# How a start-up path and two transposes are carried: DMA or TensorE, in an attention kernel with a SiLU feed-forward

## The chip, the cores and the metric

The kernel runs on one core of a Trainium2 chip. The metric is the device time of one execution in microseconds. A time is the median of several runs, and a profile is one execution recorded by the hardware profiler.

Engines are called by short names: PE (TensorE, matrix products and transposes into PSUM), DVE (VectorE), ACT (ScalarE), POOL (GpSimd) and SP (SyncE, which here only issues DMAs). Each engine works through its own list of instructions in order, and semaphores tie the lists together. PEld is the weight load of PE, which overlaps its products.

## The reference

Inputs r, k, v have the shape (4 batches, 8 heads, 768 steps, 48), w and u (8 heads, 48); the feed-forward weights w_in are 384x2048 and w_out 2048x384, all in float32.

```
state = 0
for t in range(S):
    cur   = einsum('bhd,bhe->bhde', u * k[t], v[t])
    y[t]  = einsum('bhd,bhde->bhe', r[t], state + cur)
    state = w[:, :, None] * state + einsum('bhd,bhe->bhde', k[t], v[t])

x = y.transpose(0, 2, 1, 3).reshape(B * S, H * D)
h = x @ w_in
out = (h * sigmoid(h)) @ w_out
```

So there is a decay w and a bonus u, one number for each head and channel, that every unit of work needs; then a feed-forward of two layers over 3072 tokens.

## The kernel before

The 768 steps are cut into 6 chunks of 128, and a *unit* is one chunk of one batch: 24 units, unit i being chunk i // 4 of batch i % 4. A unit goes through these steps (functions in the code):

- `load(i)`: three DMAs on SP's queue bring r, k and v of the unit into slot i % 6 (`NIN` is 6), time on the partitions. A later unit's load reuses the slot.
- `p1(i)` (units 0 to 3) or `p1t` and `p1d` (later units): PE transposes r and k so that channels lie on the partitions, and DVE multiplies them by powers of w (`lamR`, `lamK`) into `rk`.
- `nat_ku`, `nat_rk` (POOL), `bonus_sum` (DVE), `bonus_vu` (POOL) or `bonus_act` (ACT): the bonus term, the row sum of r·k·u times v, called `vu`.
- `p2(i)`: PE multiplies k by r for the even and odd heads (`ae`, `ao`), and DVE masks the result into `am`.
- `p3y`, `p3e`: PE forms y from `am`, v and the state; DVE adds `vu` and writes `y16` in float16.
- `sums`, `state`, `half_state`, `nat_kc`, `r16`: the state that is carried to the next chunk.
- `p4(i)`: y16 is turned so that channels lie on the partitions (`xT`), as the feed-forward needs them.

The feed-forward of a chunk is `l1` (16 column tiles of w_in, three products each, then Silu on ACT into `gT`) and `l2` (per batch 16 products in four parts, a DVE copy `osb`, a store on SP's queue). These pieces stand in a list, `fillers`, and `fill(n)` takes pieces worth n from it and puts them between the steps of a unit, so that PE has work while the attention's short steps wait for each other. For chunk 1 the first layer is done in two halves: units 4 and 5, then units 6 and 7 (`l1s(1, 2, 4)`, entered behind unit 7's steps).

The order of the instructions on every engine is the order in which the program is written out by hand (`manual_schedule`). The ramp of units 0 to 5 is written step by step (lines 413 to 558); from unit 6 on there is a loop (lines 559 to 594).

What matters for the start: w is read as columns, channels on the partitions, by two DMAs of 4-byte elements (line 83). DVE doubles it seven times into all its powers (lines 141 to 148). u is read by one DMA that repeats its 384 numbers on all 128 partitions (line 87), between k and v of unit 0. `spin` issues products of zeros that nothing reads. The four parts of w_in and the two of w_out are brought by POOL's queue, which converts them to float16 (`win_part`, `wout_part`); the first one is held back by a POOL copy `gate` that reads r of unit 1 (line 424), and the loads of units 4 and 5 by a POOL memset in their slot (line 451).

What matters for units 6 and 7: `p4` turns y16 by three PE transposes and an ACT copy for units 0 to 7 (lines 334 to 338), and by a DMA transpose on SP's queue from unit 8 on (line 331). In the loop, units 6 and 7 issue the loads of units 12 and 13 ahead of `p3y` (lines 570 and 571); later units issue theirs behind `p4` (lines 580 and 581).

Of the kernel before, what the change touches and what calls it, by code (L numbers as in the profile page):

```python
# [8 lines left out]
FP = mybir.dt.float32  # L9
# [6 lines left out]
def kernel(  # L16
# [47 lines left out]
    def load(i, mid=None):  # L64
        if i >= NU:
            return
        sc, b = unit(i)
        for t, src in ((rin, r), (kin, k), (vin, v)):
            if t is vin and mid:
                mid()  # L70
            nc.sync.dma_start(out=t[i % NIN][:, :, 0:D],
                              in_=src[b, :, sc * C:sc * C + C, :]
                              .rearrange("h t d -> t h d"))

    wcol = cst.tile([PR, NP], FP)
    u_bc = cst.tile([128, H, D], FP)
    junk = cst.tile([128, 512], F16)
    nc.vector.memset(junk, 0.0)  # L80
    nc.vector.memset(wcol[32:64, :], 1.0)
    for j, e in ((0, nc.sync), (1, nc.scalar)):
        e.dma_start(out=wcol[64 * j:64 * j + D, :],
                    in_=bass.AP(tensor=w.tensor, offset=D * j, ap=[[1, D], [PW, NP]]))

    def load_u():
        nc.sync.dma_start(out=u_bc.rearrange("t h d -> t (h d)"),
                          in_=bass.AP(tensor=u.tensor, offset=0, ap=[[0, 128], [1, HD]]))

    load(0, mid=load_u)  # L90
    for i in range(1, B):
        load(i)
    for t in (rin, kin):
# [25 lines left out]
    def spin(n, t=None):  # L119

        if t is None:
            t = ps.tile([128, 512], FP, name="spin", tag="t", bufs=5)
        else:
            t = t.rearrange("s p t -> s (p t)")
        for _ in range(n):
            nc.tensor.matmul(t, junk[:, 0:128], junk, start=True, stop=True)

    spin(10)
    lamC = cst.tile([128, H, D], FP)

    def to_rows(dst, cols):

        t = ps.tile([128, NP, 2, 64], FP, name="rows", tag="t", bufs=5)
        for p in range(NP):
            nc.tensor.transpose(t[:, p, :, :].rearrange("t j d -> t (j d)")[:, 0:PR],
                                cols(p), ident[0:PR, 0:PR])
        nc.scalar.copy(out=dst.rearrange("t (p j) d -> t p j d", j=2), in_=t[:, :, :, 0:D])


    wT = wcol  # L140
    nc.vector.tensor_copy(out=pi[:, 0:NP, 1:2], in_=wT.unsqueeze(2))
    nc.vector.reciprocal(out=pi[:, NP:2 * NP, 1:2], in_=wT.unsqueeze(2))
    n = 1
# [22 lines left out]
    def nat_ku(i):  # L166
        L = live.setdefault(i, {})
        L["ku"] = wrk.tile([128, H, D], FP, name="ku")
        nc.gpsimd.tensor_tensor(out=L["ku"], in0=kin[i % NIN][:, :, 0:D], in1=u_bc,  # L169
                                op=ALU.mult)  # L170

    def nat_rk(i):
        L = live[i]
        L["rku_f"] = wrk.tile([128, H, D], FP, name="rku_f")
        nc.gpsimd.tensor_tensor(out=L["rku_f"], in0=rin[i % NIN][:, :, 0:D], in1=L["ku"],  # L175
                                op=ALU.mult)
# [6 lines left out]
    def bonus_sum(i):  # L183
        L = live[i]
        L["rku"] = wrk.tile([128, H], FP, name="rku", bufs=3)
        nc.vector.tensor_reduce(out=L["rku"], in_=L["rku_f"], axis=mybir.AxisListType.X,  # L186
                                op=ALU.add)
# [12 lines left out]
            nc.scalar.activation(out=L["vu"][:, h, :], in_=vin[i % NIN][:, h, :],  # L200
                                 func=AF.Copy, scale=L["rku"][:, h:h + 1])

    def p1(i, spins=0):
        n = i % NIN
        L = live.setdefault(i, {})
        tr = ps.tile([128, NP, C], FP, name="tr", tag="t", bufs=5)
        tk = ps.tile([128, NP, C], FP, name="tk", tag="t", bufs=5)
        spin(spins, tr)
        for t, src in ((tr, rin), (tk, kin)):
            flat = src[n].rearrange("p h d -> p (h d)")  # L210
            for p in range(NP):
                nc.tensor.transpose(t[0:PR, p, :], flat[:, 128 * p:128 * p + PR], ident)
        rk = wrk.tile([PR, 2, NP, C], FP, name="rk")
        L["rT"] = rk[:, 0]
        L["kT"] = rk[:, 1]
        step = NP // 2 if i == 0 else NP
        for q in range(0, NP, step):
            q = slice(q, q + step)
            for x, t, lam_ in (("rT", tr, lamR), ("kT", tk, lamK)):
                nc.vector.tensor_tensor(out=L[x][:, q], in0=t[0:PR, q], in1=lam_[:, q],  # L220
                                        op=ALU.mult)

    def p1t(i):

# [100 lines left out]
    def p4(i):  # L325
        sc, b = unit(i)
        L = live[i]
        if sc not in xts:
            xts[sc] = wrk.tile([128, NQ, B, C], F16, name="xT", bufs=3)
        if i >= 2 * B:  # L330
            nc.sync.dma_start_transpose(out=xts[sc][:, :, b, :],
                                        in_=L["y16"].rearrange("p h d -> p (h d)"))
            return
        yT = ps.tile([128, NQ, C], F16, name="yT", tag="t", bufs=5)
        yf = L["y16"].rearrange("p h d -> p (h d)")
        for q in range(NQ):
            nc.tensor.transpose(yT[:, q, :], yf[:, 128 * q:128 * q + 128], ident16)
        nc.scalar.copy(out=xts[sc][:, :, b, :], in_=yT)
# [58 lines left out]
            f()  # L397


    zero = junk[0:PR, 0:HD].rearrange("r (p c) -> r p c", p=NP)  # L400
    gate = cst.tile([128, 1], FP)

    def win_part(c0, c1):
        nc.gpsimd.dma_start(out=win[:, :, c0:c1],  # L404
                            in_=moe_w_in[:, c0:c1].rearrange("(q p) n -> p q n", p=128))
# [4 lines left out]
            in_=moe_w_out[1024 * g:1024 * g + 1024, :].rearrange("(f p) n -> p f n", p=128))  # L410


    p1(0)
    nat_ku(0)
    nat_rk(0)
    p2(0)
    nat_v(0)
    lamCT = cst.tile([PR, NP, C], FP)
    for p in range(NP):
# [3 lines left out]
    nc.scalar.copy(out=st[0], in_=zero)  # L423
    nc.gpsimd.tensor_copy(out=gate, in_=rin[1][:, 0, 0:1])
    win_part(0, 512)
    p1(1, spins=1)
    bonus_sum(0)
    nat_ku(1)
# [3 lines left out]
    to_rows(lamC, lambda p: lamCT[:, p, :])  # L432
    bonus_act(0)
    nc.scalar.copy(out=st[1], in_=zero)
    bonus_sum(1)
    bonus_vu(1)
    win_part(512, 1024)
    p2(1, spins=2)
    p3e(0)
    spin(4)  # L440
# [118 lines left out]
    for i in range(B + 2, NU):  # L559
        sc, b = unit(i)  # L560
        if i == B + 2:
            p2(i, nxt=i + 1)
        bonus_sum(i)
        bonus_vu(i)
        if i > B + 2:
            p2(i, nxt=i + 1 if i + 1 < NU else None)
        fill(2)
        if i + 1 < NU:
            front(i + 1)
        if NIN <= i < 2 * B:  # L570
            load(i + NIN)
        fill(1)
        p3y(i)
        p3e(i)
        if sc < NCH - 1:
            sums(i)
            state(i)
        fill(2)
        p4(i)
        if i >= 2 * B:  # L580
            load(i + NIN)
        if i + 1 < NU:
            r16(i + 1)
        if i == B + 2:
            half_state(3)
        fill(1)
        if sc == 1:
            half_state(b)
        fill(1 if sc in (2, 3) else 2)
        if b == B - 1:  # L590
            if sc == 1:
                fillers.extend(l1s(1, 2, 4) + l2s(1))
            else:
                fillers.extend(l1s(sc) + l2s(sc))
# [32 lines left out]
```

## Time and profile before

| | |
|---|---|
| median of 6 runs | 200.38 us (199.85 to 201.04) |
| profiled execution | 200.22 us, its span 198.5 us |
| PE, PEld busy | 190.3 us (96%), 127.8 us (64%) |
| DVE, ACT, POOL busy | 115.9, 91.4, 115.0 us |
| DMA moved | 24.12 MB, mean 121 GB/s |
| loads of r, k, v | 24 each, 192 KB, 3.5 to 3.6 us from issue to landing (median) |
| parts of w_in | 4, 6.8 us from issue to landing (median) |
| load of u | 1, 192 KB on the chip, 4.7 us |
| loads of w | 2, 0.8 KB each, 1.8 us |
| DMA transposes | 16, 2.4 us (median) |

A row of a timeline gives the start and the duration in us, the engine, the line of the code, the operation, the tiles written and read, and in brackets the idle time before it with what ended it. SPq and POOLq are the queues on which SP and POOL issue DMAs; the duration of such a row is the issue and not the transfer. Times count from the start of the span.

### The profile page before, as it was taken

Reading aid. Unit: us, or ns where it says so; the run is one execution under the profiler, and the core shown is the slowest. Engines: PE = TensorE matmul, PEld = TensorE weight load, DVE = VectorE, ACT = ScalarE, POOL = GpSimd, SP = SyncE. Lnnn points to the kernel's source line nnn. Section 1 sums busy time; section 2 is a strip of 40 time slices with the busy share of each in tenths; the row PEclk is TensorE's granted clock in tenths of the full one; section 3 lists DMA queues with packets and bytes.
Section 4 is the critical chain, followed back from the end, with each engine's and each line's share of the span. In section 5 each row is a group of like instructions: output and inputs, shape, how many; then the busy total and the mean of one; then the engine's idle time right before and its main releaser. Section 6 shows DMA issues by size and latency. Waiting matters only on the chain.

```text
span 198.5 us, 4920 instructions
## 1 busy us (share of the span) xinstructions
PE 190.3 (96%) x1920; PEld 127.8 (64%) x1920; DVE 115.9 (58%) x234; ACT 91.4 (46%) x207; POOL 115.0 (58%) x145
## 2 busy tenths in 40 slices
PE   7889999998999999999999999999999999999993
PEld 2657778787766876766566766557656556644562
DVE  7687648895758747875675686476576344210121
ACT  2375487798331662206862216672116680069300
POOL 3489959989956885696669657735437710000000
PEclk9999999999999999999999999999999999999999
DMA  4899999999799883665666387530321011210022
GB/s 88 172 177 229 180 205 190 195 187 191 154 215 205 200 177 78 141 162 125 136 122 138 100 181 159 102 60 0 106 59 43 20 21 43 91 47 0 3 79 81
DMA packets 89400, 24.12 MB, mean 121 GB/s; under 512 B 82464, under 2 KB 89376, under 8 KB 89376
## 3 DMA queue, kind: packets, MB, share of 16 engines
q1 hardware_dynamic: 85488, 20.65, 48.1%
q0 software_dynamic: 3680, 3.15, 10.4%
q8 instruction: 15, 0.25, 0.5%
q14 instruction: 9, 0.07, 0.1%
q10 hardware_dynamic: 208, 0.00, 0.1%
HBM read 20.65 MB, written 4.72 MB: 128 GB/s over the span
## 4 chain that ended last, share of the span: by engine, by line
PE 74%; POOL 13%; issue 4%; DVE 3%; DMA 2%; ACT 1%; SPq 1%; POOLq 0%; DVEq 0%
PE ops L361 31%; PE hps L349 24%; PE ae L258 9%; PE xs L233 4%; POOL ku L169 4%; POOL rku_f L175 3%; DMA u_bc<-in_u_dram 2%; POOL kc L180 2%; PE y L284 2%; POOL vu L192 2%; PE y L281 2%; POOL win L404 2%; PE ops L375 1%; PE sps L300 1%; ACT gT L352 1%
## 5 line engine op out<-in xcount | busy, mean ns | idle before, releaser
L352 ACT ACTIVATE gT<-hps 128x256 f16<-128x256 f32 (+1 forms) x128 | 59.7, 492 | 47.1 <-PE hps L349 45.3
L349 PE MATMUL hps<-xT,win 128*128 128x256 f16 (+1 forms) x384 | 69.4, 326 | 1.1 <-ACT gT L352 0.7
L361 PE MATMUL ops<-wout,gT 128*128 128x384 f16 x368 | 64.0, 326 | 0.0
L349 PEld LDWEIGHTS <-win 128*128 128x128 f16 x384 | 35.4, 98 | 24.1 <-DMA win<-in_moe_w_in_dram 1.2
L361 PEld LDWEIGHTS <-gT 128*128 128x128 f16 x368 | 34.6, 98 | 22.3
L267 DVE TENSOR_TENSOR am<-ae,maskM 128x512 f16<-128x512 f32 x24 | 16.6, 691 | 35.1 <-PE ao L260 35.0
L365 DVE COPY osb<-ops 128x384 f32<-128x384 f32 x23 | 12.7, 554 | 27.5 <-PE ops L361 27.3
L258 PEld LDWEIGHTS ae<-rk 48*128 48x128 f32 x192 | 23.2, 187 | 8.2 <-issue 4.8
L258 PE MATMUL ae<-rk 48*128 48x128 f32 x192 | 27.9, 285 | 0.5 <-DVE rk L220 0.5
L169 POOL TENSOR_TENSOR ku<-kin,u_bc 128x384 f32<-128x384 f32 x24 | 24.2, 1006 | 7.4 <-DMA u_bc<-in_u_dram 5.0
L260 PE MATMUL ao<-rk 48*128 48x128 f32 x192 | 27.9, 285 | 0.0
L250 ACT CAST rT<-rk 112x512 f16<-112x512 f32 x20 | 12.3, 616 | 32.1 <-DVE rk L244 32.1
L192 POOL TENSOR_TENSOR vu<-vin,rku 128x384 f32<-128x384 f32 x23 | 19.1, 829 | 13.8 <-DVE rku L186 13.7
L244 DVE TENSOR_TENSOR rk<-xs,pif 112x512 f32<-112x512 f32 x40 | 25.6, 681 | 2.1 <-PE xs L233 2.1
L175 POOL TENSOR_TENSOR rku_f<-rin,ku 128x384 f32<-128x384 f32 x24 | 24.1, 1004 | 1.9
L180 POOL TENSOR_TENSOR kc<-kin,lamC 128x384 f16<-128x384 f32 x24 | 24.0, 1000 | 0.0
L260 PEld LDWEIGHTS ao<-rk 48*128 48x128 f32 x192 | 23.2, 187 | 0.0
L314 POOL CAST stb<-st 112x384 f16<-112x384 f32 x12 | 6.0, 503 | 22.2 <-DVE st L309 22.2
L291 DVE TENSOR_TENSOR y<-y,vu 128x384 f16<-128x384 f32 x24 | 13.4, 557 | 7.8 <-PE y L284 2.8
L267 DVE TENSOR_TENSOR am<-ao,maskM 128x512 f16<-128x512 f32 x24 | 16.3, 681 | 0.0
L164 ACT CAST v<-vin 128x384 f16<-128x384 f32 x24 | 12.2, 508 | 6.2 <-DMA vin<-in_v_dram 6.2
L186 DVE TENSOR_REDUCE rku<-rku_f 128x8 f32<-128x384 f32 x24 | 13.2, 551 | 2.3 <-POOL rku_f L175 1.9
(65 smaller groups left out, 172.0 us busy)
## 6 DMA issues: line engine op xcount, KB each, us to landing
rin<-in_r_dram SPq DMA_DIRECT2D x24, 192.0 KB, 3.5
kin<-in_k_dram SPq DMA_DIRECT2D x24, 192.0 KB, 3.6
vin<-in_v_dram SPq DMA_DIRECT2D x24, 192.0 KB, 3.6
out_dram<-osb SPq DMA_DIRECT2D x23, 192.0 KB, 1.9
win<-in_moe_w_in_dram POOLq DMA_DIRECT2D x4, 384.0 KB, 6.8
wout<-in_moe_w_out_dram POOLq DMA_DIRECT2D x2, 768.0 KB, 11.1
xT<-y SPq DMA_TRANSPOSE x16, 2.4
u_bc<-in_u_dram SPq DMA_DIRECT2D x1, 192.0 KB, 4.7
```

What stands on the lines that cost most here:

```text
L169: nc.gpsimd.tensor_tensor(out=L["ku"], in0=kin[i % NIN][:, :, 0:D], in1=u_bc, op=ALU.mult)
L175: nc.gpsimd.tensor_tensor(out=L["rku_f"], in0=rin[i % NIN][:, :, 0:D], in1=L["ku"], op=ALU.mult)
L180: nc.gpsimd.tensor_tensor(out=kc[i % NKC][:, :, 0:D], in0=kin[n][:, :, 0:D], in1=lamC, op=ALU.mult)
L192: nc.gpsimd.tensor_tensor(out=L["vu"], in0=vin[i % NIN], in1=L["rku"].unsqueeze(2).broadcast_to([128, H, D]), op=ALU.mult)
L244: nc.vector.tensor_tensor(out=rk[:, :, :, 64 * g:64 * g + 64], in0=xs[g][0:PR], in1=lam(g), op=ALU.mult)
L258: nc.tensor.matmul(ae[:, p, :], L["kT"][0:D, p, :], L["rT"][0:D, p, :], start=True, stop=True)
L260: nc.tensor.matmul(ao[:, p, :], L["kT"][64:PR, p, :], L["rT"][64:PR, p, :], start=True, stop=True)
L267: nc.vector.tensor_tensor(out=am, in0=a, in1=maskM.unsqueeze(1).broadcast_to([128, NP, C]), op=ALU.mult)
L291: nc.vector.tensor_tensor(out=L["y16"], in0=L["y"], in1=L["vu"], op=ALU.add)
L349: nc.tensor.matmul(hps, win[:, q, ft * 128:(ft + 1) * 128], xts[sc][:, q, b0:b1, :].rearrange("p b t -> p (b t)"), start=(q == 0), stop=(q ...
L352: nc.scalar.activation(out=gts[sc][:, ft, b0 * C:b1 * C], in_=hps, func=AF.Silu)
L361: nc.tensor.matmul(ops, gts[sc][:, ft, b * C:(b + 1) * C], wout[:, ft, :], start=(ft == 0), stop=(ft == NFT - 1))
```

## The change

It has four parts.

1. w and u are each read as rows (4 partitions of 2 x 48 numbers, padded to 64 with ones) by one DMA on SP's queue. w is turned into columns by one PE transpose, and DVE reads it from PSUM. u is turned into columns by one PE transpose, copied to SBUF by ACT, spread to all 128 partitions by four PE transposes of a broadcast column (`to_rows`), and copied into `u_bc` by ACT. These stand between the two DVE products of `p1(0)`. Of the ten first start-up products nine are left, five ahead of w's transpose and four behind it.
2. `p1(0)` writes r and then k in one DVE operation each, where unit 0 took two halves of each before.
3. In the ramp, `nat_ku(0)`, `nat_rk(0)` and `p2(0)` stand behind the gate and the first part of w_in; the second part of w_in stands ahead of `bonus_sum(1)` and `bonus_vu(1)`.
4. Units 6 and 7 are turned by a DMA transpose too, and the loads of units 12 and 13 are issued behind it.

```diff
-    wcol = cst.tile([PR, NP], FP)
-    u_bc = cst.tile([128, H, D], FP)
+    wrow = cst.tile([NP, 2, 64], FP)
+    urow = cst.tile([NP, 2, 64], FP)
     junk = cst.tile([128, 512], F16)
     nc.vector.memset(junk, 0.0)
-    nc.vector.memset(wcol[32:64, :], 1.0)
-    for j, e in ((0, nc.sync), (1, nc.scalar)):
-        e.dma_start(out=wcol[64 * j:64 * j + D, :],
-                    in_=bass.AP(tensor=w.tensor, offset=D * j, ap=[[1, D], [PW, NP]]))
-
-    def load_u():
-        nc.sync.dma_start(out=u_bc.rearrange("t h d -> t (h d)"),
-                          in_=bass.AP(tensor=u.tensor, offset=0, ap=[[0, 128], [1, HD]]))
-
-    load(0, mid=load_u)
+    for t in (wrow, urow):
+        nc.vector.memset(t[:, :, D:64], 1.0)
+
+    def load_row(t, src):
+        nc.sync.dma_start(out=t[:, :, 0:D], in_=bass.AP(tensor=src.tensor, offset=0,
+                                                        ap=[[PW, NP], [D, 2], [1, D]]))
+
+    load_row(wrow, w)
+    load(0, mid=lambda: load_row(urow, u))
...
-    spin(10)
+    def to_cols(row, copy):
+        t = ps.tile([128, 512], FP, name="cols", tag="t", bufs=5)
+        nc.tensor.transpose(t[0:PR, 0:NP], row.rearrange("p j d -> p (j d)")[:, 0:PR],
+                            ident[0:NP, 0:NP])
+        if copy is None:
+            return t[0:PR, 0:NP]
+        c = cst.tile([PR, NP], FP, name="cols_sb")
+        copy(out=c, in_=t[0:PR, 0:NP])
+        return c
+
+    spin(5)
+    wT = to_cols(wrow, None)
+    spin(4)
+    u_bc = cst.tile([128, H, D], FP)
...
-    wT = wcol
...
-    def p1(i, spins=0):
+    def p1(i, mid=None, spins=0):
...
         L["rT"] = rk[:, 0]
+        nc.vector.tensor_tensor(out=L["rT"], in0=tr[0:PR], in1=lamR, op=ALU.mult)
+        if mid:
+            mid()
         L["kT"] = rk[:, 1]
-        step = NP // 2 if i == 0 else NP
-        for q in range(0, NP, step):
-            q = slice(q, q + step)
-            for x, t, lam_ in (("rT", tr, lamR), ("kT", tk, lamK)):
-                nc.vector.tensor_tensor(out=L[x][:, q], in0=t[0:PR, q], in1=lam_[:, q],
-                                        op=ALU.mult)
+        nc.vector.tensor_tensor(out=L["kT"], in0=tk[0:PR], in1=lamK, op=ALU.mult)
...
-        if i >= 2 * B:
+        if i >= NIN:
             nc.sync.dma_start_transpose(out=xts[sc][:, :, b, :],
...
+    def to_cols_u():
+        t = to_cols(urow, nc.scalar.copy)
+        to_rows(u_bc, lambda p: t[:, p:p + 1].broadcast_to([PR, 128]))
...
-    p1(0)
-    nat_ku(0)
-    nat_rk(0)
-    p2(0)
+    p1(0, mid=to_cols_u)
     nat_v(0)
...
     win_part(0, 512)
+    nat_ku(0)
+    nat_rk(0)
+    p2(0)
     p1(1, spins=1)
...
     nc.scalar.copy(out=st[1], in_=zero)
+    win_part(512, 1024)
     bonus_sum(1)
     bonus_vu(1)
-    win_part(512, 1024)
     p2(1, spins=2)
...
-        if NIN <= i < 2 * B:
-            load(i + NIN)
         fill(1)
         p3y(i)
...
         p4(i)
-        if i >= 2 * B:
+        if i >= NIN:
             load(i + NIN)
```

## The prediction

> **What bounds the kernel now.** I read the page's busy line first, then the table of 10 us windows, then the chain that ended last, and last the timelines of TensorE (PE) and of SyncE's queue (SP) around the two places that the change touches.
>
> ```profile
> PE 190.3 (96%) x1920; PEld 127.8 (64%) x1920; DVE 115.9 (58%) x234; ACT 91.4 (46%) x207; POOL 115.0 (58%) x145
> ```
>
> ```profile
> 10.00:20.00 10.00, 9.08 (x92) 6.23 (x92) 8.02 (x14) 6.57 (x21) 9.13 (x12) 1.00 1.18 202
> 20.00:30.00 10.00, 9.28 (x114) 7.93 (x115) 5.65 (x11) 6.57 (x21) 7.49 (x9) 1.00 1.09 194
> ...
> 40.00:50.00 10.00, 9.41 (x115) 7.67 (x114) 7.08 (x16) 8.93 (x26) 9.11 (x11) 1.00 1.25 189
> 50.00:60.00 10.00, 10.00 (x121) 7.12 (x120) 6.23 (x13) 3.15 (x8) 7.80 (x10) 1.00 0.95 187
> ```
>
> Columns: stretch, length, busy time of PE, weight loads, DVE, ACT and POOL, granted clock, DMA share, GB/s. From 50 us on PE has no gap, so whatever moves PE's position at 50 to 65 us moves the end by as much. Before 50 us PE idles 0.92 + 0.72 + 0.59 + 0.59 us in the four windows from 10 us: no gain in the ramp can exceed these 2.8 us. The last-but-one column says that the DMA engines are full all that time.
>
> ```profile
> 2.89 4.66 DMA u_bc<-in_u_dram
> 7.70 1.01 POOL ku L169
> ...
> 9.91 0.87 POOL win L404
> 10.80 1.02 POOL ku L169
> 11.90 1.00 POOL rku_f L175
> 12.90 0.63 issue
> ```
>
> This is the chain's start (start, length, what): u lands at 7.55, POOL makes the bonus products of units 0 and 1 until 12.90, and only then can DVE reduce rku of unit 1, mask am of unit 1 and let PE go on at 14.75.
>
> ```profile
> 14.75 0.35 PE L284 MATMUL y<-v,am 128*128 128x48 f16 x7 [0.40 <-DVE am L267]
> ...
> 26.27 0.83 PE L349 MATMUL hps<-xT,win 128*128 128x256 f16 x6 [0.46 <-ACT gT L352]
> ...
> 48.18 0.34 PE L337 MATMUL yT<-ident,y 128*128 128x128 f16 x3 [0.52 <-DVE y L291]
> ...
> 63.98 0.82 PE L349 MATMUL hps<-xT,win 128*128 128x256 f16 x6
> ```
>
> The wait in brackets is PE's idle time before that row. At 26.27 the ACT result named was one of three buffers in turn and not the last thing to come: the landing records put the fourth part of w_in at 26.22, the third at 24.03 (PE resumes at 24.08 after 0.15 idle). At 48.18 PE waits for unit 6's output only to transpose it. At 63.98 PE starts the first layer for units 6 and 7, the first reader of what they transposed.
>
> ```profile
> 58.83 0.78 SPq L367 DMA_DIRECT2D out_dram<-osb  x1
> ...
> 64.41 1.32 SPq L331 DMA_TRANSPOSE xT<-y  x1
> ```
>
> ```profile
> DMA to landing us min/median/max: 2.3/2.4/4.2
> ```
>
> SP is late here: unit 8's output is ready at 62.7, its transpose is issued at 64.41. The last line is issue to landing of the 16 transposes that already go by DMA.
>
> **The sum is made against the profiled execution**, 200.22 us (span 198.5 and 1.7 around it); the median of the six runs is 0.16 above it, which I add back at the end.
>
> **1. w.** Removed: two column loads (one on SP, one on ACT); SP's waited until 1.34 for the memset of rows 32 to 64, ACT's went at 0.80. Added: one row load on SP with nothing to wait for (taken at 0.80, landing 1.8 later like wcol, 2.6), two small memsets on DVE (0.06 each by the wcol memset), one PE transpose. One of ten start-up products goes; five at the 0.43 us pitch seen from 1.66 to 4.65 end at 3.4, so the load is covered and w is in PSUM at about 3.75 where DVE had it at 3.31. DVE's power chain (0.17 + 0.17 + 2.39) then ends near 6.5 instead of 5.99. Cover: the first transposed r, which in before arrived at 6.65. Four more products end at 5.3, r's transposes need 0.85 + 0.2 and arrive at 6.4. Cost 0 to 0.1 on DVE; if the cover were gone, the 0.5.
>
> **2. u.** Removed: one load of 128 packets (128 ns each in the packet records: 1.02 us of all 16 DMA engines) and its SP issue of 0.68. Added: a row load (0.4 of SP), one transpose, one ACT copy of 112x4 (0.20, by the 128x1 activation), four transposes of 112 columns (0.58, by those of lamC), one ACT copy (0.47, by lamC). PE ends k's transposes at about 7.1, then 7.35, 7.6, 8.2, and u_bc is complete at 8.75 instead of 7.55. PE's products ae of unit 0 queue behind these transposes: they start at 8.1 and end at 9.1, against 7.83 with a gap and 9.21. Queued behind the two copies on ACT are v16 of unit 0 and the four lamCT activations (1.8 us, done at 10.6 against 10.02); lamC's transposes read them at 10.76, so 0.1 of cover is left.
>
> **3. p1(0)** in two DVE operations (0.68 each) instead of four (0.42 each): 0.3 less DVE, but the first product needs all of k. Hidden behind point 2.
>
> **4. Orders on POOL.** The gate copy and the first w_in part go ahead of ku and rku_f of unit 0. The gate waits for r of unit 1, which lands at 9.04 now; with u's 1.02 us gone and SP 0.5 us earlier it lands at 7.5. So the 0.87 us issue falls into the wait for u_bc; ku goes at 8.8, and four products (2.1 us a unit) end at 13.0 against 12.90. If the gate came only at 9.0, they would end at 14.0. The second w_in part goes ahead of vu of unit 1, into the 0.63 us that POOL idles at 12.90; vu ends at 14.7 against 14.40, and its reader y of unit 1 starts at 15.2. What follows on POOL comes 0.4 us earlier. PE at 14.75: +0.1 (bounds -0.1 and +0.7, the second if ACT's or PE's steps of point 2 take half as long again).
>
> **5. DMA freed.** The engines are full from 3 to 26 us, so a load less (1.02) and an earlier start (0.5) bring the third and fourth w_in part 1 to 1.5 us earlier, and with them k of unit 4 (27.65). The waits of 0.15 and 0.46 at 24.08 and 26.27 go; late next is ACT's gT, some 0.1 us behind. Taken: -0.5 (bounds 0 and -0.6). POOL's wait for k of unit 4 (2.4 us) shrinks too, but PE was not waiting for that.
>
> **6. Units 6 and 7.** Off PE: six transposes, 0.17 us per three at their pitch, so 0.34, and the wait of 0.52 at 48.18, since the next products of the first layer need nothing of unit 6. Late next would be the buffers of hps, freed by gT at 47.4 and 47.7: no wait over 0.1. Off ACT: two copies of 0.48, no gain there (ACT idles 4.8 us at 56). Taken -0.86 (bounds -0.34 and -0.9).
>
> **7. What the queue makes of it.** On SP the transposes stand behind the loads of units 10 and 11 and, for unit 7, behind unit 12's three loads and the first output store; both outputs are long ready (48.1 and 55.1), so SP waits for no semaphore, it only is late. Behind them stand the loads of units 12 and 13 (three DMAs each, 2.6 us later at most, first read at 79 and 85), then two stores (four buffers, the fifth store is at 77.92) and unit 8's transpose (read at 88): all covered. In before the store issued at 58.83 had its first engine landed at 61.3 and its last at 63.3, one engine being behind. Two transposes add 0.46 each (packet time of the 16 over 16); earlier DMAs take 1.0 to 1.5 off. So unit 7's transpose lands between 61 and 64.2, and I take 62.9: nearest to the row just ahead of it, with one engine late. PE wants it at 63.98 + 0.1 - 0.5 - 0.86 = 62.7. Taken +0.3 (bounds 0 and +1.5).
>
> Sum: 0 + 0.1 - 0.5 - 0.86 + 0.3 = -0.96, say -0.9. From the profiled 200.22 that is 199.3; on the median's scale 200.38 - 0.9 = **199.5 us**.
>
> **A rule weighed.** The first start-up products run at a pitch of 0.43 us, those at 12.87 at 0.22, and r's first transposes take 418 ns where the median is 273: PE is at half pace until about 7.1 us. The Trainium skill, "TensorE: Matmul & The Clock Gate", Parts 1 and 4, says that the clock opens after a busy window of about 3.4 us that runs free of the kernel, and that transposes do not count as busy. By the rows the ramp stays as it is, since PE is occupied as before (sum -0.9); by the rule one product less and five transposes more could cost a window of 3.4 us at half pace, an estimate of some +1.7 us before what waits absorb. I go by the rows and keep the case as a rival.
>
> **Rivals.**
> - *A: unit 7's transpose comes late* (the other side). If the DMA lead of point 5 is used up by 60 us and SP pays both issues in full (1.3 each), it is issued at 61.2 to 62 and lands by the slower of its rows (3 to 4.2) at 64.4 to 65.5. PE would then start at 63.98 + 0.4 to 1.5: 200.8 to 201.8, say 201.1. It decides from a landing at 64.6. For it: SP is already 1.7 us late at 64.41; against: DMA has a load less.
> - *B: u_bc or the gate comes late*, +0.7 at 14.75 instead of +0.1, and the w_in waits no longer matter: 200.1. For it: five more steps across three engines; against: each has a row.
> - *C: the clock opens one window later* (3.4 us after 7.1). PE issues 2.2 us between 7.8 and 10.6 now; doubled, with DVE's chain behind, about +1.0 at 14.75, or +1.7 if more falls in it: 200.5 to 201.2.
> - *D: unit 7's transpose lands before PE comes and all w_in waits go*: -1.4, 199.0.
>
> **How the numbers follow.** A time is told from no change by about 0.3%, 0.6 us. Forecast 0.37, D 0.08: faster 0.45. B 0.20 and the lower half of C 0.08: within 0.28. A 0.20 and the upper half of C 0.07: slower 0.27. The forecast's own range is 199.0 to 199.9; the range over the cases leaves out the ends of D and A: 198.7 to 201.4.
>
> **What would show it.** ku of unit 0 at 8.8 and rku_f of unit 1 ending near 13.0; no gap of PE at 24.1 and 26.3; PE past unit 6 with no wait near 47.5; 18 DMA transposes; PE's first product for units 6 and 7 near 62.9, with a wait for xT of 0 to 0.5. Wrong it would be if that wait is over 1.5 us (A), if ku of unit 0 starts after 9.4 (B), or if the products of unit 0 at 8 us are 0.2 apart instead of 0.11 (C).

## The result and the profile after

The changed kernel takes 198.37 us (median of 21 runs, 198.00 to 200.35) where the kernel before, run beside it, takes 200.13 (47 runs, 199.10 to 201.37): a ratio of 0.9922, 95% interval 0.9906 to 0.9938. That is 1.56 us less by the ratio, which goes by means, and 1.76 less by the medians. The forecast was 0.9 less, 199.5 us, and its range began at 198.7. The direction was right and the size too small.

Of the 21 runs, 18 lie between 198.0 and 198.7 (their median is 198.37 too) and three between 199.8 and 200.4; the profiled execution, 199.94 us (span 198.2), comes beside them and is of the second kind, so it shows a wait that most runs can't have in full.

The page's busy line and the table of windows of the changed kernel:

```profile
PE 189.2 (95%) x1919; PEld 126.9 (64%) x1919; DVE 115.4 (58%) x233; ACT 91.1 (46%) x207; POOL 115.0 (58%) x145
```

```profile
10.00:20.00 10.00, 8.82 (x91) 5.95 (x89) 7.84 (x14) 5.80 (x19) 9.82 (x13) 1.00 1.06 181
20.00:30.00 10.00, 9.84 (x119) 8.23 (x119) 6.11 (x12) 6.95 (x22) 7.72 (x9) 1.00 1.13 203
...
40.00:50.00 10.00, 10.00 (x124) 8.33 (x123) 6.71 (x15) 8.89 (x26) 9.08 (x11) 1.00 1.24 192
50.00:60.00 10.00, 10.00 (x115) 6.83 (x112) 7.63 (x14) 1.99 (x4) 8.78 (x10) 1.00 0.88 174
60.00:70.00 10.00, 8.58 (x112) 6.99 (x111) 6.40 (x14) 4.30 (x12) 5.33 (x7) 1.00 0.90 207
```

PE's idle time has shrunk from 0.72 to 0.16 us at 20 to 30 us and from 0.59 to nothing at 40 to 50 us; at 10 to 20 it has grown a little, from 0.92 to 1.18. And there are now 1.42 us at 60 to 70, where PE had none. The timelines of POOL and of PE say which waits these are. First the changed kernel:

```profile
7.68 0.19 POOL L434 COPY gate<-rin 128x1 f32<-128x1 f32 x1 [4.96 <-DMA rin<-in_r_dram]
7.81 0.93 POOL L417 DMA_DIRECT2D win<-in_moe_w_in_dram  x1
8.76 1.02 POOL L180 TENSOR_TENSOR ku<-kin,u_bc 128x384 f32<-128x384 f32 x1
...
11.90 1.00 POOL L186 TENSOR_TENSOR rku_f<-rin,ku 128x384 f32<-128x384 f32 x1
```

```profile
14.75 0.35 PE L293 MATMUL y<-v,am 128*128 128x48 f16 x7 [0.40 <-DVE am L276]
...
25.53 0.81 PE L358 MATMUL hps<-xT,win 128*128 128x256 f16 x6
...
27.31 0.43 PE L242 MATMUL xs<-ident,rin 64*112 64x64 f32 x8
...
45.65 2.13 PE L358 MATMUL hps<-xT,win 128*128 128x256 f16 x18
47.61 1.46 PE L370 MATMUL ops<-wout,gT 128*128 128x384 f16 x8
...
56.41 0.37 PE L267 MATMUL ae<-rk 48*128 48x128 f32 x1
...
64.01 0.81 PE L358 MATMUL hps<-xT,win 128*128 128x256 f16 x6 [1.42 <-DMA xT<-y]
```

Then three rows of PE in the kernel before, to set against those at 27.31, 47.61 and 56.41:

```profile
27.85 0.43 PE L233 MATMUL xs<-ident,rin 64*112 64x64 f32 x8
...
49.01 1.46 PE L361 MATMUL ops<-wout,gT 128*128 128x384 f16 x8
...
57.98 0.37 PE L258 MATMUL ae<-rk 48*128 48x128 f32 x1
```

POOL now waits for r of unit 1 and not for u, and its chain ends at the same 12.90. PE stands where it stood at 14.75. At 25.53 (26.27 before) there is no wait any more, and unit 4's transposes start at 27.31 instead of 27.85: 0.54 earlier. Near 47 us the wait for unit 6's output is gone, and the first `ops` starts at 47.61 instead of 49.01, so another 0.86 beside the 0.54. Unit 8's `ae` starts at 56.41, where it was 57.98, so 1.57 us are gained by then, 1.03 of them by units 6 and 7. PE would reach the first layer of units 6 and 7 at about 62.4 (35.10 us behind unit 4's transposes, as in the kernels below that don't wait). It starts at 64.01, and the row names unit 7's transpose. SP's timeline shows where that one was:

```profile
55.71 1.63 SPq L340 DMA_TRANSPOSE xT<-y  x1
57.46 0.51 SPq L71 DMA_DIRECT2D rin<-in_r_dram  x1
58.06 1.59 SPq L71 DMA_DIRECT2D kin<-in_k_dram  x1
59.76 0.52 SPq L71 DMA_DIRECT2D vin<-in_v_dram  x1
60.37 0.62 SPq L376 DMA_DIRECT2D out_dram<-osb  x1
61.09 1.18 SPq L340 DMA_TRANSPOSE xT<-y  x1
```

SP's rows follow each other without a pause. Unit 7's output is ready at 53.7 (the end of DVE's row for its y); its transpose is issued 7.4 us later, behind unit 12's loads and a store.

One more difference stands at the very end. The last row of DVE, before and then after, with the spans 198.5 and 198.2 us:

```profile
195.24 0.29 DVE L379 COPY osh<-ops 128x128 f32<-128x128 f32 x1 [0.47 <-PE ops L375]
```

```profile
195.26 0.29 DVE L388 COPY osh<-ops 128x128 f32<-128x128 f32 x1 [0.47 <-PE ops L384]
```

The engines end their work at the same time, but the program ends 0.3 us sooner: 2.94 us after the start of that row, where it was 3.26. What is left there is the last store and the program's end.

### The profile page after: what moved, and what is told of

Read it like the earlier page. It is cut to its first block, busy times and chain, and to the rows that moved or that the text cites. A ratio compares the mean times of both kernels' runs of the same rounds, so it can differ in the third digit from the quotient of the medians.

```text
span 198.2 us, 4920 instructions
## 1 busy us (share of the span) xinstructions
PE 189.2 (95%) x1919; PEld 126.9 (64%) x1919; DVE 115.4 (58%) x233; ACT 91.1 (46%) x207; POOL 115.0 (58%) x145
## 4 chain that ended last, share of the span: by engine, by line
PE 82%; DVE 5%; issue 4%; POOL 3%; ACT 1%; DMA 1%; POOLq 0%; DVEq 0%
PE hps L358 29%; PE ops L370 29%; PE ae L267 11%; PE xs L242 4%; PE y L293 3%; DVE am L276 2%; PE y L290 2%; DMA xT<-y 1%; PE sps L309 1%; PE ops L384 1%; POOL rku_f L186 1%; POOL ku L180 1%; DVE y L300 1%; ACT gT L361 1%; PE yT L346 1%
## 5 line engine op out<-in xcount | busy, mean ns | idle before, releaser
L325 POOL TENSOR_TENSOR sdec<-st,pif 112x384 f32<-112x384 f32 x16 | 13.3, 836 | 1.1 <-ACT gT L361 1.1
```

## The experiments

Diffs are against the changed kernel unless another is named. "Unit 4's transposes" are the rows `xs<-ident,rin` near 27 us: their start measures the length of the ramp. Their start and the wait for `xT` (PE's idle time ahead of the first layer of units 6 and 7) are from the one profiled execution of each kernel; ratios are against the kernel before on the same chip, with 95% intervals.

| kernel | ratio | unit 4's transposes | PE's wait for xT |
|---|---|---|---|
| before (three profiles) | 1 | 27.85, 28.17, 28.03 | none |
| changed (three profiles) | 0.9922, 0.991, 0.9908 | 27.31, 27.13, 27.41 | 1.4, 0.5, 1.8 |
| ramp alone (parts 1 to 3) | 0.9938 | 27.11 | none |
| part 4 alone, on before | 1.0006 | 29.03 | 1.5 |
| unit 7's transpose first | 0.9864, 0.9856 | 27.47, 27.14 | none |
| unit 6 alone by DMA | 0.9876 | 27.25 | none |
| unit 7's transpose on ACT | 0.9906 | 26.91 | none |
| dead load of u, ahead of the gate's input | 1.0015 | 30.59 | none |
| dead load behind unit 1's loads | 1.0004 | 28.44 | 1.7 |
| POOL's old order | 0.9931 | 27.73 | 0.6 |
| old order and dead load | 1.0005 | 28.31 | 0.4 |
| transpose first, w by columns | 0.9893 | 27.45 | none |

### The ramp alone, and the transposes alone

The first undoes part 4 in the changed kernel:

```diff
-        if i >= NIN:          # in p4
+        if i >= 2 * B:
...
+        if NIN <= i < 2 * B:
+            load(i + NIN)
...
-        if i >= NIN:          # behind p4(i) in the loop
+        if i >= 2 * B:
             load(i + NIN)
```

> Parts 1 to 3 alone: units 6 and 7 are turned by TensorE as before. By the sum of the prediction (freed DMA, and nothing at 14.75 us) 0.5 us faster than before, with TensorE's row at 48.18 near 47.6 and its wait of 0.5 for unit 6's output still there. The rival (the ramp gives nothing that lasts, all of the 1.6 us is units 6 and 7): within 0.2 us of before.

The second makes the same edit the other way round in the kernel before.

> Part 4 alone on the kernel before: units 6 and 7 turned by DMA, u and w loaded as before. If the lead that the freed DMA time gives is not needed: 1.0 us faster, no wait for xT. If it is needed (rival): TensorE wants unit 7's output at 63.0 and the transpose lands at 64 or later, so a wait of 1 us or more eats the gain and the kernel is within 0.4 us of before.

Measured: the ramp alone takes 199.80 us, ratio 0.9938 (0.9916 to 0.9960), so some 1.2 us of gain without part 4, more than the 0.5 expected. Part 4 alone takes 201.70, ratio 1.0006 (0.9971 to 1.0041): nothing, as its rival said. Its profile shows the gain made and given back: at the first layer of units 6 and 7

```profile
66.10 0.81 PE L349 MATMUL hps<-xT,win 128*128 128x256 f16 x6 [1.47 <-DMA xT<-y]
```

PE waits 1.47 us for the transpose that SP issued at 63.30. It waits 0.28 for a part of w_out at 52.62 as well. Turning both units is worth 1.46 us on the same chip (199.80 to 198.34) where the ramp is short and unit 7's transpose comes first, as shown next. So the parts are not additive by themselves.

These 1.46 us are 1.03 on PE up to the first layer of units 6 and 7, and 0.4 at the end of the program. From the start of DVE's last row to the end of the span, the four profiles without part 4 (three of the kernel before, one of the ramp alone) take 3.26 to 3.40 us, the twelve with both units turned by DMA 2.84 to 2.97, and the one with unit 6 alone 3.02. So this belongs to part 4 too. Why the program's end is shorter, no run here shows.

The ramp-alone kernel also shows what the wait for unit 6's output really costs. Its PE timeline there:

```profile
45.45 1.47 PE L358 MATMUL hps<-xT,win 128*128 128x256 f16 x12
47.44 0.34 PE L346 MATMUL yT<-ident,y 128*128 128x128 f16 x3 [0.52 <-DVE y L300]
47.62 0.82 PE L358 MATMUL hps<-xT,win 128*128 128x256 f16 x6
48.27 1.46 PE L370 MATMUL ops<-wout,gT 128*128 128x384 f16 x8
```

From the start of these 18 products to `ops` it needs 48.27 - 45.45 = 2.82 us; the changed kernel needs 47.61 - 45.65 = 1.96. The difference, 0.86, is 0.17 for the three transposes and 0.69 for a wait that the bracket gives as 0.52. A product of this form is 0.27 long at a pitch of (2.13 - 0.27) / 17 = 0.11; the bracket counts from the end of the last product, and without the wait the next one would start 0.16 ahead of that end. PE's wait for `xT` shows the same: 64.01 is 1.60 behind 62.41, and the bracket says 1.42.

### Unit 7's transpose ahead of unit 12's loads

```diff
-        if i >= NIN:
+        if i == NIN + 1:
+            load(i + NIN - 1)
+        if i > NIN:
             load(i + NIN)
```

> The changed kernel, with unit 7's transpose put ahead of unit 12's three loads on SP's queue (both units' loads behind it). If the queue ahead of it is what makes it late in the profiled execution (199.94 against the median 198.37): no wait for xT in the profile either, the profiled run near 198.3 like the others, median 198.3. The rival (the wait comes from the transpose itself or from the profiler's recording): the wait of 1.4 us stays in the profiled run.

Measured: 198.34 us (198.16 to 198.49), ratio 0.9864 (0.9839 to 0.9890). PE doesn't wait for `xT`. Later it was run beside the changed kernel and two further variants on another chip: unit 7 turned by PE again (`i >= NIN and i != NIN + 1` in `p4`), and unit 7's transpose issued by ACT (`nc.scalar if i == NIN + 1 else nc.sync`).

> The changed kernel beside the next three on one chip, so that they can be set against it. Theory: PE waits for unit 7's transpose between 0 and 1.7 us, by how late SP issues it (60.5 us: 0.5 waited; 61.1: 1.4; 62.8 with everything 1.1 later: 1.7, in the profiles so far); 0.8 to 1.1 % under the kernel before. Rival (the wait is the transfer's own length, whatever the issue): the landing comes 3 us or more behind the issue in one profile and under 2 in another.

> Unit 7's transpose ahead of unit 12's loads, again, now on the chip of the changed kernel. Theory (the queue ahead of it makes the wait): issued near 57.5, no wait for xT at 62.4, and 0.4 to 1.2 us under the changed kernel's median, by how much that one waits on this chip. Rival (the loads that now come later hurt unit 12): PE waits for rin or kin of unit 12 near 79, and the same time as the changed kernel's.

> The changed kernel with unit 7's output turned by PE again; the loads stay where the change puts them. Theory: PE pays three transposes and no wait for unit 7 (0.17 by point 6; 0.17 measured between 47.6 and 56.5), and is free of the wait for its DMA: first products of units 6 and 7 at 62.5 to 62.7 with no wait; 198.2 to 198.6 where the kernel before takes 200.1, so 0.1 to 0.2 over the kernel with the transpose put first, and level with or 0.2 to 0.8 under the changed kernel. Rival (unit 7's PE transposes wait for y as unit 6's did, 0.5): +0.7 against the kernel with the transpose first.

> The changed kernel with unit 7's transpose issued by ACT, where nothing stands ahead of it, in place of SP. Theory (SP's order is what made it late, not the transfers of the loads): issued at 53.5 to 54.5, landed before 59, no wait for xT; as fast as the kernel with the transpose first (within 0.3), or 0.2 to 0.4 slower if ACT's issue of about 1.2 us holds up gT. Rival (transposes wait for the transfers ahead of them on the DMA engines): it lands past 62.4 although issued near 54, and the wait of up to 1.7 stays.

Measured, the kernel before at 201.10:

| | median us | runs | ratio |
|---|---|---|---|
| changed | 199.00 | 198.34 to 200.40 | 0.9908 (0.9878 to 0.9937) |
| unit 7's transpose first | 198.18 | 198.03 to 198.27 | 0.9856 (0.9835 to 0.9876) |
| unit 6 alone by DMA | 198.55 | 198.48 to 198.72 | 0.9876 (0.9856 to 0.9897) |
| unit 7's transpose on ACT | 198.87 | 198.24 to 199.92 | 0.9906 (0.9876 to 0.9936) |

The kernel with the transpose first, SP's timeline and then PE's:

```profile
54.76 1.47 SPq L340 DMA_TRANSPOSE xT<-y  x1
56.32 0.52 SPq L376 DMA_DIRECT2D out_dram<-osb  x1
56.94 2.59 SPq L340 DMA_TRANSPOSE xT<-y  x1
```

```profile
62.24 0.82 PE L358 MATMUL hps<-xT,win 128*128 128x256 f16 x6
```

Issued at 56.94 and not 61 to 62, unit 7's transpose has landed when PE comes; in its eight runs on two chips there is no second group 1.6 us up. In four of the seven profiles that do wait, SP's issue and PE's restart are 60.47 and 62.91, 61.09 and 64.01, 61.89 and 64.51, 63.30 and 66.10: 2.4 to 2.9 us apart, over an issue that moves by 2.8. The other three lie between (2.5 to 2.6). So the wait is set by when SP gets to the transpose, and the rival (the length of the transfer) falls. Unit 12's loads, now later, are waited for nowhere.

With unit 6 alone by DMA, PE pays three transposes for unit 7 with no wait ahead of them and reaches the first layer at 62.52: 35.27 us after unit 4's transposes, against 35.10 with both by DMA. So of the 1.03 us unit 6 is worth 0.86 and unit 7 0.17. Its median is 0.37 over that of the transpose first, more than the 0.1 to 0.2 expected and less than the rival's 0.7; its waits show nothing of the rival's kind. The two profiles are 0.4 apart: 0.17 for the transposes, 0.11 in the ramp, 0.12 at the program's end.

The variant on ACT missed its expectation. It was to issue at 53.5 to 54.5, and did so at 57.78, as the timeline of ACT and its queue shows:

```profile
57.78 1.28 ACTq L340 DMA_TRANSPOSE xT<-y  x1
59.10 0.62 ACT L259 CAST rT<-rk 112x512 f16<-112x512 f32 x1 [9.27 <-DVE rk L253]
```

Unit 6's transpose, issued by SP at 54.74, had a landing time of 2.9 us, so it was there at 57.64. ACT, idle since 49.83, waits for it in the program and issues its own transpose behind it; that took 4.3 us and landed at 62.1, just ahead of PE at 62.29. PE doesn't wait for `xT` in the profiled run, but the detour has a price: ACT's cast `rT` of unit 8 stands behind the transpose and runs at 59.10 (in the changed kernel at 52.77), and y of unit 8, which reads it, starts 32.87 us behind unit 4's transposes where it is 32.59 with the transpose first. So PE is 0.28 late. Two of the six runs took 199.9, and why was not profiled. The Trainium skill, "DMA: Bandwidth & Descriptors", section "DMA Transpose (X-bar)", says that transposes of two issuing engines must not be in flight together and that the later has to wait until the earlier is complete; the 57.64 and 57.78 agree with it. Moving the transpose to an idle engine's queue did not take it out of the queue of transposes here.

### The load of u put back, and POOL's order

A load of u into all partitions that nobody reads gives back the DMA work that the change took away, and leaves the rest of the change:

```diff
+    u_dead = cst.tile([128, H, D], FP)
+    def load_dead():
+        load_row(urow, u)
+        nc.sync.dma_start(out=u_dead.rearrange("t h d -> t (h d)"),
+                          in_=bass.AP(tensor=u.tensor, offset=0, ap=[[0, 128], [1, HD]]))
-    load(0, mid=lambda: load_row(urow, u))
+    load(0, mid=load_dead)
```

> The changed kernel with the broadcast load of u put back as a dead load into a tile that nothing reads, behind the row load of u. It costs the 1.02 us of the DMA engines and 0.68 us of SP's issue again. If the freed DMA time carries the gain of the ramp: 0.5 us slower than the changed kernel (1.1 faster than before) when unit 7's transpose still comes in time, and up to 2 us slower where it does not. The rival (the gain of the ramp comes from the order on POOL's queue): within 0.2 us of the changed kernel.

Measured: 201.59 us, ratio 1.0015 (0.9990 to 1.0041). One load of 1.02 us (its packet time over the 16 engines) costs the whole gain of all four parts, where 0.5 was expected, and up to 2 us if unit 7's transpose came late, which it doesn't in its profile. POOL's timeline, then PE's, then PE's table of windows (stretch, length, PE busy, granted clock, DMA share, GB/s):

```profile
9.68 0.19 POOL L441 COPY gate<-rin 128x1 f32<-128x1 f32 x1 [6.95 <-DMA rin<-in_r_dram]
...
13.89 1.00 POOL L193 TENSOR_TENSOR rku_f<-rin,ku 128x384 f32<-128x384 f32 x1
```

```profile
16.13 0.20 PE L300 MATMUL y<-v,am 128*128 128x48 f16 x1 [1.88 <-DVE am L283]
16.73 0.35 PE L300 MATMUL y<-v,am 128*128 128x48 f16 x7 [0.40 <-DVE am L283]
```

```profile
16.00:17.00 1.00, 0.47 (x9) 1.00 1.32 171
17.00:18.00 1.00, 1.00 (x10) 0.54 1.03 165
18.00:19.00 1.00, 1.00 (x7) 0.50 1.23 196
19.00:20.00 1.00, 1.00 (x7) 0.50 1.20 226
20.00:21.00 1.00, 1.00 (x7) 0.76 1.05 203
```

r of unit 1 lands 2.0 us later than in the changed kernel (9.68 to 7.68), the gate stands ahead of the bonus products, and everything behind it moves by those 2 us: PE goes on at 16.73 instead of 14.75. The wait of 1.88 us then closes the clock: (0.46 + 0.50 + 0.50 + 0.24) / 0.5 = 3.4 us at half pace, and unit 4's transposes come 3.28 us later than in the changed kernel's first profile, 1.3 of it from the clock (16.73 to the next row of that form, 23.39, takes 6.66 us; 14.75 to 20.11 takes 5.36 in the changed kernel). By the run times the clock is worth less: three of the ten runs have a mean clock of 1.00 and took 200.32, 201.24 and 201.51, the other seven have 0.991, as the profiled one, and took 201.69 on average, 0.67 more. So most of the loss stands without it. Two questions remained: is it the gate or the load, and is the order on POOL worth anything? One run puts the dead load behind unit 1's loads, past the gate's input. Two put POOL's old order back, without and with the dead load in its first place:

```diff
+    nat_ku(0)
+    nat_rk(0)
     nc.gpsimd.tensor_copy(out=gate, in_=rin[1][:, 0, 0:1])
     win_part(0, 512)
-    nat_ku(0)
-    nat_rk(0)
     p2(0)
...
-    win_part(512, 1024)
     bonus_sum(1)
     bonus_vu(1)
+    win_part(512, 1024)
```

> The changed kernel itself, timed beside the next three on one chip. Theory (the wait for unit 7's transpose belongs to a part of its executions): most times about 1.6 us under the kernel before and a few at its level, nothing between; in a profiled execution PE's first product of units 6 and 7 at 62.4 without a wait, or at 63.9 to 64.1 after one of 1.4. Rival (the first chip's second group was a chance of that chip): one group only, 1.5 to 1.8 us under.

> The changed kernel with a load of u into all partitions (nobody reads it) behind unit 1's loads, so that the gate's input is in front of it: only the DMA time is taken back, not the gate. Theory (the freed DMA time is worth the 0.5 us of point 5, and 3.2 us of the earlier dead load were the gate's): ku of unit 0 stays at 8.8, PE at 14.75, then waits for w_in of 0.2 to 0.5, xs(4) at 27.8 instead of 27.31; in all +0.3 to +0.6 us over the changed kernel. Rival (1 us of DMA costs 1 us or more wherever it stands, since the engines are full): +1.0 to +1.5.

> The changed kernel with POOL's order of before: ku and rku_f of unit 0 ahead of the gate, the second w_in part behind vu of unit 1. Theory (POOL makes five steps until 12.9 in either order, so the order alone gives nothing before 14.75; it only sends w_in 1.9 us earlier): first w_in part issued at 9.7, rku_f(1) ends at 12.8 or earlier, PE at 14.75, xs(4) at 27.3 to 27.6: +0 to +0.3 us over the changed kernel. Rival (w_in's early issue is what brought the 0.5): waits of 0.15 and 0.5 for w_in near 24 and 26 as before, xs(4) at 27.85, +0.5.

> POOL's order of before, and the dead load of u in its old place: against the earlier run of the dead load (3.2 us slower than the changed kernel) only the order differs. Theory (the gate in front of POOL's bonus products is what made the load cost 3.2): with two products ahead of it the gate waits for nothing, rku_f(1) ends at 12.9, PE goes on at 14.75, the clock stays open, xs(4) at 27.9; +0.5 to +0.9 over the changed kernel. Rival (the load itself costs it, by the transfers behind it): +2.5 or more, with PE's waits for rin and win instead of for am.

Measured, the kernel before at 200.80: the changed kernel 199.21 (198.82 to 199.46), ratio 0.9910 (0.9880 to 0.9940), in one group this time, and with a wait of 0.52 in its profile that the theory of two groups with nothing between had no place for; the late dead load 1.0004 (0.9967 to 1.0042); the old order 199.45, ratio 0.9931 (0.9904 to 0.9959); the old order with the dead load 1.0005 (0.9960 to 1.0050).

With the load late the gate is where it was (7.67), ku(0) at 8.76 and PE at 14.74, as the theory said. But then, on PE's timeline:

```profile
16.51 0.65 PE L227 MATMUL tk<-ident,kin 128*112 128x128 f32 x4 [0.54 <-DMA kin<-in_k_dram]
...
28.44 0.43 PE L246 MATMUL xs<-ident,rin 64*112 64x64 f32 x8
```

PE waits for k of unit 2, and the ramp is 1.31 us longer than in the changed kernel's profile on the same chip (27.13). That is the rival's 1.0 to 1.5 and not the theory's 0.5. SP's whole list moves back with it, unit 7's transpose is issued at 62.81 and waited for 1.7 us instead of 0.5, so that the time is longer by more than either said: 1.9 us by the ratios.

The old order without the load lengthens the ramp by 0.6 (27.73 against 27.13): ku(0) starts at 8.12 and the gate copy and w_in's issue, 1.1 us, stand between the products again, so rku_f(1) ends at 13.33 against 12.72. In the medians it is 0.24 us, inside the theory's 0 to 0.3, though its rows (12.8, 14.75) were missed; PE doesn't wait for w_in, so the rival falls. With the load on top the ramp grows by another 0.58, and these waits of PE come back:

```profile
10.01 0.65 PE L230 MATMUL tr<-ident,rin 128*112 128x128 f32 x4 [0.58 <-DMA rin<-in_r_dram]
...
26.73 0.83 PE L365 MATMUL hps<-xT,win 128*128 128x256 f16 x6 [0.69 <-DMA win<-in_moe_w_in_dram]
...
28.31 0.44 PE L249 MATMUL xs<-ident,rin 64*112 64x64 f32 x8
```

Only the second one lengthens the ramp: y of unit 1 stands at 15.09 with the load and at 15.17 without. So the same load costs the ramp 0.6 us in POOL's old order, 1.3 behind the gate's input in the new one, and 3.3 ahead of it. The gate is most of the 3.3, as the theory said, but the load has a price of its own everywhere. By the ratios all three kernels with the load stand at the level of the kernel before. For the last the theory was 0.5 to 0.9 over the changed kernel and the ratios make it 1.9; its profile, 199.86 us, was its quickest run, so it explains less than the ratio shows. What the later runs of these kernels did is open: none of them was profiled.

### The ramp of the kernel before, and w

The kernel before was profiled twice more, and w was read by columns again on top of the kernel with the transpose first:

```diff
-    load_row(wrow, w)
+    nc.vector.memset(wcol[32:64, :], 1.0)
+    for j, e in ((0, nc.sync), (1, nc.scalar)):
+        e.dma_start(out=wcol[64 * j:64 * j + D, :],
+                    in_=bass.AP(tensor=w.tensor, offset=D * j, ap=[[1, D], [PW, NP]]))
...
-    spin(5)
-    wT = to_cols(wrow, None)
-    spin(4)
+    spin(10)
+    wT = wcol
```

> The kernel before, profiled a second time. Theory (with the broadcast of u in front of the loads the ramp's length varies from execution to execution): PE's transposes of unit 4 start anywhere from 27.8 to 29.1, later by what r or k of unit 1, or w_in, lands later. Rival (its ramp is fixed and only the chips differ): 27.85 within 0.15 again, and the same waits of 0.4 and 0.46.

> The kernel before, profiled a third time, on the same chip as the second. Theory: differs from the second by 0.3 us or more at unit 4's transposes. Rival: within 0.15 of the second.

> The kernel with unit 7's transpose put first, with w read as columns by two DMAs again (u still by rows). Point 1 said 0 to 0.1 us for w. Theory (w's part is worth nothing, u's is): gate at 7.6 to 7.9, ku of unit 0 by 9.0, unit 4's transposes at 27.0 to 27.5, 0.985 to 0.988 of the kernel before as with the row load. Rival (SP's wait for the memset until 1.3 sends every load half a microsecond later, and that is much of the gain): gate at 8.2 or later, unit 4's transposes at 27.7 to 28, and 0.4 to 0.6 us slower.

Measured: 200.65 and 200.38 us in the two profiles, with unit 4's transposes at 28.17 and 28.03. The second profile's PE:

```profile
8.91 0.65 PE L212 MATMUL tr<-ident,rin 128*112 128x128 f32 x4 [0.29 <-DMA rin<-in_r_dram]
...
24.34 1.48 PE L349 MATMUL hps<-xT,win 128*128 128x256 f16 x12 [0.60 <-DMA win<-in_moe_w_in_dram]
26.59 0.83 PE L349 MATMUL hps<-xT,win 128*128 128x256 f16 x6 [0.52 <-DMA win<-in_moe_w_in_dram]
...
28.17 0.44 PE L233 MATMUL xs<-ident,rin 64*112 64x64 f32 x8
```

Two profiles on one chip that differ by 0.14 are not what the theory asked for (0.3), and 28.17 is not what its first rival asked for (27.85 within 0.15); the second rival, within 0.15 of each other, holds. With the part-4-alone kernel, whose ramp is that of the kernel before, there are four profiles of this ramp: 27.85, 28.03, 28.17 and 29.03. The changed ramp has eight, from 26.91 to 27.47. The ranges don't overlap, the means are 28.27 and 27.22, and the profile that the prediction was made from was the shortest of its four. They come from several chips, so whether the chip or the execution makes the difference within a group can't be told.

Where the difference between the groups lies can be told. From the row of y with the wait of 0.40 (14.75 in the first profiles) to unit 4's transposes, all eight profiles of the changed ramp take 12.56 or 12.57 us, and the four of the ramp before 13.10, 13.30, 13.61 and 13.69. In that stretch stand the waits for the third and fourth part of w_in, and their brackets add up to 0.61 (0.15 and 0.46 in the first profile), 0.80, 1.12 (0.60 and 0.52 here) and 1.19, in the same order. Up to the row of y the two groups overlap: 14.56 to 15.34 before, 14.34 to 14.90 after. The waits for r and k of unit 1 lie in that first part, and the second profile has them and still reaches y earliest of its group (14.56). So what the freed DMA time gives in every profile is the w_in waits, 0.53 to 1.13 us.

w by columns: 198.55 us, ratio 0.9893 (0.9850 to 0.9937), gate at 7.53, unit 4's transposes at 27.45, no wait for `xT` and none for w_in. SP starts 0.54 later for the memset (1.35 instead of 0.81), but its row load takes 0.84 to issue and the column load 0.40, so r of unit 0 is issued at 1.81 against 1.71. The rival falls; whether w's part is worth 0 or a few tenths can't be told from these runs.

## Why the prediction was right or wrong

The sum was made against the profiled execution, so it can be set against the two first profiles, term by term:

| term | forecast | the two first profiles |
|---|---|---|
| points 1 to 4, PE at 14.75 | +0.1 | 0.0 |
| point 5, DMA freed, to unit 4's transposes | -0.5 | -0.54 |
| point 6, units 6 and 7 off PE, to unit 8's `ae` | -0.86 | -1.03 |
| point 7, wait for unit 7's transpose | +0.3 | +1.60 in this execution |
| end of the program | not in the sum | -0.32 |

With the wait the right column gives -0.29, and the spans went from 198.5 to 198.2. Without the wait it gives -1.89, and 200.22 less 1.89 is 198.33: the 18 quicker runs have a median of 198.37. So the steps that failed are two. Point 7 charged +0.3 for a wait that most runs can hardly have, and the sum left the program's end out, at nothing, where part 4 saves 0.3 to 0.4. Points 4 and 6 add 0.1 and 0.17 to the miss. That the quicker runs don't wait is argued from their times and not seen: a profile of this kernel always showed some wait.

- **Point 1 (w, 0 to 0.1 on DVE) and points 2 and 3 (u, p1):** right in the sum, not in the steps. u_bc was ready at 7.67 and not 8.75, because r's first transposes ran at 5.02 to 5.62 at their full pace in this execution, and SP's lead was 0.1 and not 0.5, since the row load of w takes 0.84 to issue. The two operations of `p1(0)` were not run by themselves.
- **Point 4 (+0.1 at 14.75):** 0.0. ku(0) came at 8.76 where 8.8 was said, but the gate set it in this execution, not u_bc: a good number by luck. That the gate's order hangs on r of unit 1 was named with "If the gate came only at 9.0, they would end at 14.0"; with the dead load it came at 9.68, and they ended at 14.89. This is rival B's mechanism, and it is there to be had for a load of 1 us; the price, 2.0 us at that row and 1.3 behind it for the clock, is far over the 0.7 that was put on it.
- **Point 5 (DMA freed, -0.5, bounds 0 and -0.6):** right against the profile it was read from (-0.54), and so were the waits named, those for the third and fourth part of w_in. But the bounds were the waits of that one execution, the shortest of four; over the eight and four profiles that stretch is 0.53 to 1.13 shorter. In the runs of the result this need not have counted: in the kernel before, everything behind unit 4's transposes takes the same 170.7 us in its three profiles (170.65 to 170.73), so a median of 200.13, 0.09 under the profiled 200.22, leaves the typical ramp near 27.8. Beside the experiments the kernel before takes 200.6 to 201.1, and the three profiles of its ramp there are longer (28.03 to 29.03): there the point's -0.5 was too small.
- **Point 6 (-0.86): mis-sized a little, -1.03.** The wait of 0.52 is worth 0.69, for the reason shown above; transposes at 0.17 a unit were right.
- **Point 7 (+0.3, bounds 0 and +1.5): right in mechanism, wrong in the value that holds most often.** In the profiled executions the bracket is 0.5, 1.4 and 1.8 us, by an issue at 60.5, 61.1 and 61.9. The three longer runs stand 1.4 to 2.0 above the others' median, which is the size of the two longer waits; a profile shows the wait only for runs of 198.82, 199.94 and 200.40.
- **Rivals.** A (unit 7's transpose late) is what the profiled execution shows, with its +1.6; it came to the size of a loss only without the ramp's part, as part 4 alone shows (1.0006). D (the transpose in time and all w_in waits gone) is nearest to most runs; its -1.4 was short by point 6 and by the program's end. C (the clock opens a window later) did not happen at the start: unit 0's products at 8 us are 0.11 apart, the mark that was set for it. The rule weighed for it did show itself elsewhere, see the last section.

## What to carry to other kernels

Where products overlap, a wait costs more than its bracket, by the product's length less its pitch (0.16 us here); and a stretch that waits for full DMA engines should be sized from several executions, on more than one chip, since one of them shows only the waits that it happened to have. Set the end of the span against the last engine's row too: 0.3 us of this change stood there and in no row. When a transfer that somebody waits for is moved to a queue, put it ahead of what nobody waits for yet: two lines that did this here are worth 0.8 us over the change on the chip where both ran, and give 198.18 us, 1.4% under the kernel before (ratio 0.9856, 0.9835 to 0.9876). A gate ahead of an engine's other work is only as early as the load that it waits for.

## What the runs showed of the hardware

- In one profile, a wait of PE of 1.88 us (with a few short products behind it) came just ahead of a granted clock of 0.50 for 3.4 us, which cost 1.3 us there. The Trainium skill, "TensorE: Matmul & The Clock Gate", Part 1, gives a window of about 3.4 us, free of the kernel, in both directions: the 3.4 us at half pace agree with it. That a whole idle window of such a length closes the clock is not what the row shows: PE was idle for 1.88 us, and had issued a full microsecond of products (13.21 to 14.25) just before; in the 3.45 us up to the drop (13.60 to 17.05) it was busy for 1.17. Waits of up to 0.77 us between 10 and 30 us left the clock at 1.00 in the profiles of the other kernels. The kernel before has a mean clock of 0.990 or 0.991 in 4 of the 57 runs beside the experiments; none of these was profiled.
- A row of SP is not of a fixed length: in the changed kernel loads took 0.4 to 5.4 us, over all kernels transposes 1.2 to 2.7, and from 43 to 64 us the rows follow each other without a pause. Whether a long row is all issue or holds a wait inside it, the rows don't show. From issue to landing a transpose took 2.3 us in the median of the changed kernel, and up to 5.0 in the profiles at 54 to 62 us.
- Two transposes on two queues went one behind the other, since the program waits between them: 57.64 landed, 57.78 issued.
